# Block 0 of an interleaved attention and MLP kernel: a later load and later statistics for the third input tile, an undivided turn of the second, and one sum step moved behind a layer norm

## The chip, the cores and the metric

One Trainium2 chip (trn2), one of its cores. The metric is the device time of one launch in microseconds, as the median of several launches. Each launch also leaves a span, from the first to the last instruction of the program in the profile. The span is about 1.7 us shorter than the time in most launches, and it scatters less. All runs count as fast at a granted TensorE clock of 1.0, except one execution that is named where it occurs.

## The reference

Four layers on a [2048, 1024] bf16 residual: attention A, MLP B, attention A, MLP B, with the same weights both times.

```python
x = x + A(layernorm(x))     # qkv = x @ wqkv; 32 heads of 32; 8 keys at distance 0, 2, .. 14; softmax; @ wo
x = x + B(layernorm(x))     # (relu(x @ W_gate) * (x @ W_up)) @ W_down, hidden size 3584
x = x + A(layernorm(x))
x = x + B(layernorm(x))
```

## The kernel before

The 2048 rows are 16 tiles of 128, four to a block of 512. The program is a list of steps with a planned moment each. The list is sorted by that moment, and this gives every engine one order of instructions. The moment itself does nothing at run time. An engine runs its instructions in order, and so does SyncE, whose instructions are nearly all the loads and stores.

The opening, with block 0. V is computed first. Tile 0's products over the first half of the contraction start as soon as tile 0 is normalised and turned by PE transposes, then tile 1's, and so on.

```python
    def load_x(b, tiles=range(TPB)):
        for t in (b * TPB + i for i in tiles):
            if t == 0:
                sp_dma(x_tiles[t][:, 0:SLAB], ...)               # SyncE's queue
                nc.scalar.dma_start(x_tiles[t][:, SLAB:D], ...)  # ACT's queue
            elif t == 2:
                nc.scalar.dma_start(x_tiles[t][:], ...)
            else:
                sp_dma(x_tiles[t][:], ...)
    load_x(0, range(TPB - 1))
    ...
    load_slab(("v0", 0), qkv_half(2, 0))     # first V slab: two loads of 512 KB
    load_x(0, [TPB - 1])
    load_slab(("v0", 1), qkv_half(2, 1))
    ...
        scratch(13)                          # PE warm-up
        bn(0, 0); bn(0, 1); aggr(0)          # DVE statistics of tile 0, power on POOL
        act_square(2); act_mean(2)           # ACT statistics of tile 2
        bn(1, 0)
        apply(0, 0); apply(0, 1)             # DVE: tile 0 normalised
        turn(0)                              # PE: 8 transposes
        copy(0, "a", 0, 0, KC // 4)          # ACT: transposes to SBUF
        copy(0, "a", 0, KC // 4, KC // 2)
        bn(1, 1); aggr(1)
        copy(0, "v", 1)                      # DVE
        act_power(2)
        apply(1, 0); apply(1, 1)
        def second(h):
            turn(1, (h,))                    # 4 transposes
            if h == 0:
                copy(1, "v", 0)
                return
            copy(1, "v", 1)
            apply(2); act_square(3); act_mean(3); act_power(3); apply(3)
        ...
        def head():
            for kc in range(KC // 2):        # 4 times 8 products of tile 0
                if kc == KC // 2 - 1:
                    ln["second"](0)
                for c in range(KC):
                    prod(kc, c, 0, 1)
            ln["second"](1)                  # then tile 1's products
```

Around 180 us, the second layer norm (LN2) of block 0 and the logit sums of block 1 (steps of a product and an addition on DVE, `sums1`) share DVE. The sums are stored to DRAM and read back in another layout. The weight slabs of the MLP come in the same SyncE queue.

```python
    spread(sums1[6:10], t_fill + 1.4, 4.6)
    ...
            ev.append((at + 37.5, store_s(1, 1)))   # store of the scores' second half, waits for DVE
            ev.append((at + 40.5, load_s(1)))       # four loads of what it stored
    # slab_events: a weight slab is queued when a place in its ring of 5 should be free
            events.append((ends[i - RING] + 0.3 if i >= RING else 0.1 * i, ...))
```

Of the kernel before, what the change touches and what calls it, by code (L numbers as in the profile page):

```python
# [13 lines left out]
P = 128  # L14
# [6 lines left out]
KC = D // P  # L21
BLK = 512
TPB = BLK // P
# [13 lines left out]
def kernel(  # L37
# [11 lines left out]
    nc = tc.nc  # L49
# [13 lines left out]
    x_dram = A_x.flatten_outer_dims()  # L63
# [102 lines left out]
    x_tiles = []  # L166
# [4 lines left out]
    def load_x(b, tiles=range(TPB)):  # L171
        for t in (b * TPB + i for i in tiles):
            if t == 0:
                sp_dma(x_tiles[t][:, 0:SLAB], x_dram[t * P:(t + 1) * P, 0:SLAB])
                nc.scalar.dma_start(x_tiles[t][:, SLAB:D], x_dram[t * P:(t + 1) * P, SLAB:D])  # L175
            elif t == 2:
                nc.scalar.dma_start(x_tiles[t][:], x_dram[t * P:(t + 1) * P, :])
            else:
                sp_dma(x_tiles[t][:], x_dram[t * P:(t + 1) * P, :])

    load_x(0, range(TPB - 1))


    slab = {}
# [117 lines left out]
        return mv, rstd  # L302

    load_slab(("v0", 0), qkv_half(2, 0))
    load_x(0, [TPB - 1])
    load_slab(("v0", 1), qkv_half(2, 1))
    load_slab(("qk01", "q", 0), qkv_half(0, 0))

# [9 lines left out]
    def ln_first():  # L318
        hold = {"xnT": xnT_pool.tile([P, TPB, KC, P], BF16, tag="xnT", name="xnT_first")}
        xna = big_tile([P, TPB, D], "xn_first", True)  # L320
        last = {}

        def on(eng, f, *args, **kwargs):
            if eng == "v":
                dv(f, *args, **kwargs)
            elif eng in last:
                with tc.issue_after(last[eng]):
                    last[eng] = f(*args, **kwargs).ins  # L328
            else:
                last[eng] = f(*args, **kwargs).ins  # L330

        def small(name, bufs=4):
            return stat_pool.tile([P, 1], F32, tag="f" + name, name=name, bufs=bufs)

        mean, rstd, bst, sq = {}, {}, {}, {}

        def bn(t, half):
            if half == 0:
                bst[t] = stat_pool.tile([P, 2, 6], F32, tag="bst", name="bst")
            on("v", nc.vector.bn_stats, bst[t][:, half, :], x_tiles[t][:, half * SLAB:(half + 1) * SLAB])  # L340

        def aggr(t):
            mv = stat_pool.tile([P, 2], F32, tag="mv", name="mv", bufs=4)
            on("v", nc.vector.bn_aggr, mv[:], bst[t][:].rearrange("p a b -> p (a b)"))
            mean[t] = mv[:, 0:1]
            power(t, mv[:, 1:2], 1.0)

        def power(t, var, sign):
            rstd[t], vpe = small("rstd1"), small("vpe1")
            on("g", nc.gpsimd.tensor_scalar, vpe[:], var, sign, EPS, op0=ALU.mult, op1=ALU.add)  # L350
            on("g", nc.gpsimd.tensor_tensor, rstd[t][:], vpe[:], neg_half[:, 0:1], op=ALU.pow)

        def act_square(t):
            sq[t] = small("sq1")
            on("a", nc.scalar.activation, xna[:, t, :], x_tiles[t][:], ACT.Square, scale=float(D) ** -0.5,
               accum_out=sq[t][:])

        def act_mean(t):
            mn = small("mean1")
            on("a", nc.scalar.activation, xna[:, t, :], x_tiles[t][:], ACT.Identity, scale=1.0 / D, accum_out=mn[:])  # L360
            mean[t] = mn[:]

        def act_power(t):
            nvar = small("nvar1")
            on("v", nc.vector.scalar_tensor_tensor, nvar[:], mean[t], mean[t], sq[t][:], op0=ALU.mult, op1=ALU.subtract)
            power(t, nvar[:], -1.0)

        def apply(t, half=None):
            cols = slice(0, D) if half is None else slice(half * SLAB, (half + 1) * SLAB)
            on("v", nc.vector.tensor_scalar, xna[:, t, cols], x_tiles[t][:, cols], mean[t], rstd[t][:],  # L370
               op0=ALU.subtract, op1=ALU.mult)

        tps = {}

        def turn(t, halves=(0, 1)):
            if t in tps:
                pass
            elif t == 0:
                tps[t] = [psum.tile([P, KC // 2, P], BF16, tag="acc", name=f"tp{h}")[:] for h in range(2)]
            else:  # L380
                both = psum_l.tile([P, 2, KC, P], BF16, tag="L", name="tp_pair")
                tps[t] = [both[:, h, 0:KC // 2, :] for h in range(2)]
            for c in (h * (KC // 2) + i for h in halves for i in range(KC // 2)):
                with pe_group():
                    tail_pe[0] = nc.tensor.transpose(tps[t][c // (KC // 2)][:, c % (KC // 2), :],  # L385
                                                     xna[:, t, c * P:(c + 1) * P], ident[:]).ins

        def copy(t, eng, h, i0=0, i1=KC // 2):
            f = nc.vector.tensor_copy if eng == "v" else nc.scalar.copy
            on(eng, f, hold["xnT"][:, t, h * (KC // 2) + i0:h * (KC // 2) + i1, :], tps[t][h][:, i0:i1, :])  # L390

        warm = small("warm")
        on("a", nc.scalar.activation, warm[:], ones[:, 0:1], ACT.Identity)
        scratch(13)
        bn(0, 0)
        bn(0, 1)
        aggr(0)
        act_square(2)
        act_mean(2)
        bn(1, 0)  # L400
        apply(0, 0)
        apply(0, 1)
        turn(0)
        copy(0, "a", 0, 0, KC // 4)
        copy(0, "a", 0, KC // 4, KC // 2)
        bn(1, 1)
        aggr(1)
        copy(0, "v", 1)
        act_power(2)
        apply(1, 0)  # L410
        apply(1, 1)

        def second(h):
            turn(1, (h,))
            if h == 0:
                copy(1, "v", 0)
                return
            copy(1, "v", 1)
            apply(2)
            act_square(3)  # L420
            act_mean(3)
            act_power(3)
            apply(3)

        hold["second"], hold["last"] = second, last
        hold["later"] = {t: (lambda t=t: (turn(t), copy(t, "a", 0), copy(t, "v", 1))) for t in (2, 3)}
        return hold

# [22 lines left out]
    def v_first(ln):  # L451
        st = att[0]
        pairs, opened = {}, set()

        def prod(kc, c, t0, t1):
            part = t0 // 2
            if (part, c // 2) not in pairs:
                pairs[part, c // 2] = psum.tile([P, 2, BLK // 2], F32, tag="acc", name="acc_v")
            acc = pairs[part, c // 2][:, c % 2, (t0 % 2) * P:(t0 % 2 + t1 - t0) * P]
            with pe_group():  # L460
                mm(acc, lhsT=slab["v0", kc // (KC // 2)][:, kc % (KC // 2), c * P:(c + 1) * P],
                   rhs=ln["xnT"][:, t0:t1, kc, :], start=(part, c // 2) not in opened, stop=(kc == KC - 1),
                   skip_group_check=True)
            opened.add((part, c // 2))

        def head():
            st["vT"] = big_tile([P, KC, BLK], "vT_0", True)
            for kc in range(KC // 2):
                if kc == KC // 2 - 1:
                    ln["second"](0)  # L470
                for c in range(KC):
                    prod(kc, c, 0, 1)
            ln["second"](1)

        def first_half(t):
            def f():
                for c in range(KC):
                    if t == 2 and c == KC // 2:
                        ln["later"][3]()
                    for kc in range(KC // 2):  # L480
                        prod(kc, c, t, t + 1)
            return f

        def second_half(i, t0):
            def f():
                if (i, t0) == (2, 0):
                    ln["later"][2]()
                for c in (2 * i, 2 * i + 1):
                    for kc in range(KC // 2, KC):
                        prod(kc, c, t0, t0 + 2)  # L490
                tail_act[0] = nc.scalar.copy(st["vT"][:, 2 * i:2 * i + 2, t0 * P:(t0 + 2) * P],
                                             pairs.pop((t0 // 2, i))[:]).ins
            return f

        tail = [(GRP * (2 + 4 * part + 0.5 * i), second_half(i, 2 * part)) for part in range(2) for i in range(KC // 2)]
        return head, [(GRP, first_half(1)), (4 * GRP, first_half(2)), (5 * GRP, first_half(3))] + tail
# [471 lines left out]
    sums1 = prod_sum_steps(1)  # L968
    spread(sums1[:4], t_pv0 + 34.5, 4.5)
    spread(sums1[4:6], t_wo0 + 0.5, 2.5)  # L970
    spread(sums1[6:10], t_fill + 1.4, 4.6)
    spread(sums1[10:], t_gu0 + 2.6, 5.4)
    spread(load_v_steps(1), t_wo0 + 4.0, 7.0)
    ev.append((t_gu0 - 0.01, start_hidden))
# [107 lines left out]
```

## Time and profile before

| | us |
|---|---|
| time, median of 3 launches (lowest, highest) | 1617.87 (1617.67, 1618.37) |
| span of the profiled launch | 1616.4 |
| the same kernel in the later rounds beside the changed one, median of all 6 | 1618.20 (highest 1619.15) |

The page of the kernel before: span, busy time of the engines, and the chain of work that ended last.

```profile
span 1616.4 us, 18930 instructions
PE 1611.3 (100%) x7633; PEld 786.6 (49%) x7633; DVE 1137.1 (70%) x960; ACT 475.8 (29%) x968; POOL 180.4 (11%) x168
...
PE 99%; DMA 0%; ACT 0%; DVE 0%; issue 0%; ACTq 0%; DVEq 0%
```

PE is busy all the time and is the whole chain. The next view lists what PE waited for (total, times, longest, us).

```profile
PE scratch L132 <- DVE ones L310: 1.5, 1, 1.5
PE acc_v L132 <- ACT xnT_first L328: 0.4, 1, 0.4
```

The view lists no other wait of PE in 1616 us. PE's timeline of the opening (start us, length us, engine, line, operation, count, and in brackets idle time and its releaser):

```profile
6.97 0.72 PE L385 MATMUL tp<-ident,xn_first 128*128 128x128 bf16 x8
8.09 1.50 PE L132 MATMUL acc_v<-xnT_first,w_v 128*128 128x128 bf16 x24 [0.40 <-ACT xnT_first L328]
9.51 0.40 PE L385 MATMUL tp_pair<-ident,xn_first 128*128 128x128 bf16 x4
9.74 0.61 PE L132 MATMUL acc_v<-xnT_first,w_v 128*128 128x128 bf16 x8
10.64 3.59 PE L132 MATMUL acc_v<-xnT_first,w_v 128*128 128x128 bf16 x47
```

The 24, then 8 products of tile 0 have tile 1's first transposes between them, and tile 1's products begin at 10.64. ACT's timeline beside it shows why the first product came at 8.09. ACT ran tile 2's mean pass and turned to the copy only then:

```profile
6.63 1.06 ACT L328 ACTIVATE xn_first<-x 128x1024 bf16<-128x1024 bf16 x1
...
7.68 0.63 ACT L328 COPY xnT_first<-tp 128x256 bf16<-128x256 bf16 x2
```

DVE at LN2 of the last tile: the variance is ready at 181.0, but one product and one addition of the sums (`t` and `ac`, 2.29 us each) stand before the tile is normalised (`xn_b`).

```profile
180.85 0.15 DVE L106 TENSOR_SCALAR vpe<-mv 128x1 f32<-128x1 f32 x1
180.93 2.29 DVE L106 TENSOR_TENSOR t<-q,k 128x2048 f32<-128x2048 bf16 x1
183.14 2.29 DVE L106 TENSOR_TENSOR ac<-ac,t 128x2048 f32<-128x2048 f32 x1
185.35 0.54 DVE L106 TENSOR_SCALAR xn_b<-x,mv,rstd 128x1024 bf16<-128x1024 bf16 x1
```

### The profile page before, as it was taken

To read this page: it belongs to the slowest core of one execution; us is meant where nothing else is said; L and a number is where in the kernel's file an instruction comes from. 1 tells how busy PE (TensorE), PEld (TensorE's weight loads), DVE (VectorE), ACT (ScalarE), POOL (GpSimd) and SP (SyncE) were. 2 spreads that over 40 slices of the span, in tenths; PEclk is the share of its full clock that TensorE was granted. 3 is DMA by queue.
4 is the path that set the end of the run, shared out by engine and by line. 5 is a ranking of instruction groups with operands and counts; after the bars stand their busy time and mean duration, and the time that the engine had idled before them with its cause. 6 is when DMAs were issued, how large, how long until landed. Compare 5 with 4: busy or idle time off the path is not lost.

```text
span 1616.4 us, 18930 instructions
## 1 busy us (share of the span) xinstructions
PE 1611.3 (100%) x7633; PEld 786.6 (49%) x7633; DVE 1137.1 (70%) x960; ACT 475.8 (29%) x968; POOL 180.4 (11%) x168
## 2 busy tenths in 40 slices
PE   9999999999999999999999999999999999999999
PEld 6646544444444445444454444544445444444444
DVE  5999989996989698929489293893939939311211
ACT  5853312132116313603136031361313311131110
POOL 2400100010003002300053000530005100000000
PEclk9999999999999999999999999999999999999999
DMA  9868868697669766794847947479574794755452
GB/s 306 180 190 238 224 159 262 183 216 204 208 192 217 200 184 212 192 246 146 227 160 201 240 153 230 152 205 252 165 226 155 203 245 157 209 161 177 157 167 68
DMA packets 407448, 317.92 MB, mean 197 GB/s; under 512 B 166464, under 2 KB 387008, under 8 KB 406848
## 3 DMA queue, kind: packets, MB, share of 16 engines
q1 hardware_dynamic: 406784, 316.13, 69.9%
q8 instruction: 59, 0.97, 0.3%
q10 hardware_dynamic: 576, 0.59, 0.1%
q14 instruction: 29, 0.24, 0.0%
HBM read 266.29 MB, written 34.66 MB: 186 GB/s over the span
## 4 chain that ended last, share of the span: by engine, by line
PE 99%; DMA 0%; ACT 0%; DVE 0%; issue 0%; ACTq 0%; DVEq 0%
PE acc_u L132 24%; PE acc_g L132 24%; PE dacc L132 18%; PE acc_v L132 7%; PE acc_wo L132 7%; PE acc_k L132 7%; PE acc_q L132 7%; PE dacc_pair L132 6%; DMA x<-in_A_x_dram 0%; ACT xn_first L328 0%; PE tp_pair L385 0%; PE L L132 0%; DVE x L837 0%; DVE xnT_first L106 0%; ACTq L175 0%
## 5 line engine op out<-in xcount | busy, mean ns | idle before, releaser
L132 PE MATMUL acc_g<-xnT_b,w_g 128*128 128x512 bf16 x1792 | 423.3, 379 | 0.0
L132 PE MATMUL acc_u<-xnT_b,w_u 128*128 128x512 bf16 x1792 | 423.3, 379 | 0.0
L790 ACT ACTIVATE r<-acc_g 128x512 bf16<-128x512 f32 x224 | 133.5, 596 | 726.7 <-PE acc_g L132 701.6
L106 DVE TENSOR_TENSOR hT<-acc_u,r 128x512 bf16<-128x512 f32 x224 | 150.5, 685 | 240.7 <-PE acc_u L132 238.2
L132 PE MATMUL dacc<-w_d,hT 128*128 128x512 bf16 (+1 forms) x1400 | 301.9, 375 | 0.0
L132 PEld LDWEIGHTS <-hT 128*128 128x128 bf16 x1820 | 178.1, 98 | 208.9
L132 PEld LDWEIGHTS <-w_u 128*128 128x128 bf16 x1792 | 175.3, 98 | 211.5
L132 PEld LDWEIGHTS <-w_g 128*128 128x128 bf16 x1792 | 175.4, 98 | 211.4
L106 DVE TENSOR_TENSOR pv<-a,vhm 128x4096 bf16<-128x4096 bf16 x64 | 143.4, 2281 | 0.0
L837 DVE TENSOR_TENSOR x<-dacc,x 128x512 bf16<-128x512 f32 (+1 forms) x38 | 24.5, 672 | 154.2 <-PE dacc L132 154.2
L608 DVE TENSOR_TENSOR t<-q,k 128x2048 f32<-128x2048 bf16 x56 | 128.0, 2292 | 6.7 <-ACT k L543 4.6
L106 DVE TENSOR_TENSOR t<-q,k 128x2048 f32<-128x2048 bf16 x56 | 127.4, 2285 | 3.7 <-ACT k L543 2.6
L106 DVE TENSOR_TENSOR pv<-pv 128x1024 bf16<-128x1024 bf16 (+1 forms) x128 | 113.6, 947 | 0.0
L549 POOL COPY kh<-k 128x14 bf16<-128x14 bf16 x40 | 56.0, 1406 | 504.3 <-ACT k L543 504.3
L132 PE MATMUL acc_wo<-w_o,oT 128*128 128x512 bf16 x512 | 111.8, 379 | 0.0
L621 DVE TENSOR_TENSOR ac<-ac,t 128x2048 f32<-128x2048 f32 x48 | 109.6, 2284 | 0.3
L106 DVE TENSOR_TENSOR ac<-ac,t 128x2048 f32<-128x2048 f32 x48 | 109.5, 2282 | 0.0
L264 POOL TENSOR_TENSOR st_b<-st_b,neg_half 128x1 f32<-128x1 f32 x29 | 43.9, 1523 | 525.8 <-ACT st_b L263 525.7
L132 PE MATMUL dacc_pair<-w_d,hT 128*128 128x512 bf16 x420 | 95.9, 379 | 0.0
L132 PEld LDWEIGHTS <-oT 128*128 128x128 bf16 x512 | 50.0, 98 | 60.4
L259 ACT ACTIVATE xn_b<-x 128x1024 bf16<-128x1024 bf16 x29 | 30.3, 1045 | 129.1 <-DVE x L106 67.0
L446 ACT CAST vT<-acc_v 128x512 bf16<-128x512 f32 x56 | 32.8, 588 | 57.6 <-PE acc_v L132 56.6
(134 smaller groups left out, 1230.0 us busy)
## 6 DMA issues: line engine op xcount, KB each, us to landing
w_g<-in_B_W_gate_dram SPq DMA_DIRECT2D x56, 1024.0 KB, 7.4
w_u<-in_B_W_up_dram SPq DMA_DIRECT2D x56, 1024.0 KB, 5.5
w_d<-in_B_W_down_dram SPq DMA_DIRECT2D x48, 1024.0 KB, 5.7
w_o<-in_A_wo_dram SPq DMA_DIRECT2D x16, 1024.0 KB, 7.0
vhm<-v_d SPq DMA_DIRECT2D x32, 284.0 KB, 6.8
v_d<-vT SPq DMA_DIRECT2D x8, 1024.0 KB, 9.8
oT<-o_d SPq DMA_DIRECT2D x32, 256.0 KB, 4.5
w_d<-in_B_W_down_dram SPq DMA_DIRECT2D x16, 512.0 KB, 3.9
```

The source lines that it names most:

```text
L106: tail_dve[0] = f(*args, **kwargs).ins
L132: tail_pe[0] = nc.tensor.matmul(*args, **kwargs).ins
L259: nc.scalar.activation(xn, xt[:], ACT.Square, accum_out=sq)
L264: nc.gpsimd.tensor_tensor(rstd, vpe, neg_half[:, 0:1], op=ALU.pow)
L446: tail_act[0] = nc.scalar.copy(st["vT"][:, c, :], acc[:]).ins
L549: nc.gpsimd.tensor_copy(khalo[n][:, c, :], k[:, BLK:BLK + HALO])
L608: nc.vector.tensor_tensor(t[:], i0, i1, op=ALU.mult)
L621: nc.vector.tensor_tensor(o, ac[:], t[:], op=ALU.add)
L790: tail_act[0] = nc.scalar.activation(rs[j][:], acc[:], ACT.Relu).ins
L837: run = dv if n < NB - 2 else (lambda f, *args, **kwargs: f(*args, **kwargs))
```

## The change

Its intent is to let ACT's copy go at once (tile 2's statistics behind it, so its load may come later), to put the V weights ahead of tile 2 in the queue, to turn tile 1 in one piece, and to free LN2's last tile from a sum step. Tile 3's statistics move from ACT to DVE.

```diff
-            elif t == 2:
-                nc.scalar.dma_start(x_tiles[t][:], x_dram[t * P:(t + 1) * P, :])
...
-    load_x(0, range(TPB - 1))
+    load_x(0, [0, 1])
...
     load_slab(("v0", 0), qkv_half(2, 0))
-    load_x(0, [TPB - 1])
+    load_x(0, [2, 3])
...
         aggr(0)
-        act_square(2)
-        act_mean(2)
...
         copy(0, "a", 0, KC // 4, KC // 2)
+        act_square(2)
+        act_mean(2)
         bn(1, 1)
         aggr(1)
         copy(0, "v", 1)
-        act_power(2)
...
-        def second(h):
-            turn(1, (h,))
-            if h == 0:
-                copy(1, "v", 0)
-                return
+        def second():
+            turn(1)
+            copy(1, "v", 0)
             copy(1, "v", 1)
+            bn(3, 0)
+            act_power(2)
+            bn(3, 1)
+            aggr(3)
             apply(2)
-            act_square(3)
-            act_mean(3)
-            act_power(3)
             apply(3)
...
             for kc in range(KC // 2):
-                if kc == KC // 2 - 1:
-                    ln["second"](0)
                 for c in range(KC):
                     prod(kc, c, 0, 1)
-            ln["second"](1)
+            ln["second"]()
...
-    spread(sums1[6:10], t_fill + 1.4, 4.6)
+    spread(sums1[6:10], t_fill + 3.3, 4.0)
```

More of the change, by code (lines that the diff above doesn't have):

```diff
@@ L373, in ln_first, with turn @@
         tps = {}
-        def turn(t, halves=(0, 1)):
-            if t in tps:
-                pass
-            elif t == 0:
+        def turn(t):
+            if t == 0:
                 tps[t] = [psum.tile([P, KC // 2, P], BF16, tag="acc", name=f"tp{h}")[:] for h in range(2)]
@@ L382, in turn @@
                 tps[t] = [both[:, h, 0:KC // 2, :] for h in range(2)]
-            for c in (h * (KC // 2) + i for h in halves for i in range(KC // 2)):
+            for c in range(KC):
                 with pe_group():
```

## The prediction

> **What bounds the kernel.** TensorE. On the page PE is busy 1611.3 of 1616.4 us and the chain that ended last is 99% PE. PE waits twice: 1.5 us before its first warm-up matmul, 0.4 us before the first V product (on ACT's copy of tile 0's transposes). After 10.6 us the timeline has no PE gap. So only the first 10.7 us can pay, or a new stall can cost.
>
> **The opening now (timeline, us).** Tile 0's first four transposes end at 7.37, but ACT is in tile 2's mean pass (6.63 to 7.69), so its copy runs 7.68 to 8.04 and V starts at 8.09. A 128-column matmul takes 0.056. After 24 V products come tile 1's first four transposes (9.50), 8 products (to 10.19), a wait for DVE's copy (9.94 to 10.36), the other transposes (10.42), and tile 1's products at 10.64.
>
> **The change there.**
> - Tile 2's load goes behind the first V slab. Loads land at about 256 KB per 0.68 us (V halves 6.74 and 8.11, tile 3 8.79), so I expect tile 1 near 4.75, V halves 6.1 and 7.4, tile 2 8.1. None was PE's last wait.
> - Tile 2's two ACT passes follow the copies: the copy starts near 7.40, V near 7.81. Gain 0.28.
> - That gain is not kept. Tile 1's normalised halves still come at 9.41 and 9.78. The 32 products end at 9.59, eight transposes give results by 10.22, and only then DVE's copy (0.42) starts: the copies of the pair tile wait for all eight (tile 3: transposes end 17.87, copy 17.90). PE has nothing to do meanwhile; today eight V products cover it. Tile 1's products start near 10.73, against 10.64. Net cost 0.1.
> - Tile 3's statistics move to DVE (two passes of 0.65), tile 2's end later: applies end near 13.5 and 14.9, for turns at 14.2 and 17.3: no stall.
>
> **The sum step.** Now a product and an addition (2.29 each, from 180.93) stand before the fourth tile's apply (185.35); POOL's power beside them takes 2.55 against 0.55 for earlier tiles. Moved, the apply comes near 181.7 and its transposing load lands near 185.5, not 188.99. PE needs it at 190.29 and does not wait today: slack, no time. DVE loses about 0.7 idling for POOL, so the first gates come at 202.2, not 201.46; PE first needs that at 204.10. No PE effect.
>
> **Sum.** -0.28 (copy earlier) +0.38 (turn no longer covered) = +0.1 us, within scatter (1617.67 to 1618.37). The Trainium skill, "DMA: Bandwidth & Descriptors" (issuing engines are not separate DMA queues), says that DMAs of different engines run on the same 16 DMA engines and interleave; the landing rate here agrees, so moving the load reorders bytes and frees none.
>
> Predicted 1617.9 us, 8 in 10 between 1617.2 and 1618.5. Faster by over 2%: 0.005; within 2%: 0.99; slower: 0.005.
>
> **Signs that I am right:** ACT copy at 7.4, V at 7.8; a new PE wait of 0.5 to 0.7 us on DVE's copy of tile 1 between 10.0 and 10.75; first Q product within 0.2 of 23.88; first gate product within 0.2 of 190.29 without a wait; POOL's fourth power 0.55.
>
> **What would make it wrong:** copies not waiting for all eight transposes (then -0.15); tile 1 normalised earlier because its load is (up to -0.4); tile 2's late statistics holding its turn at 14.2 (up to +0.7); DVE's delay reaching PE's accumulators near 204 (+0.5).

## More of the kernel before

Last, DMA traffic between 3.5 and 6.0 us, by queue (packets, MB, share of 16 engines). q1 is SyncE's queue and q10 is ACT's.

```profile
DMA packets 539, 0.98 MB, mean 393 GB/s; under 512 B 51, under 2 KB 67, under 8 KB 539
...
q1 hardware_dynamic: 384, 0.72, 78.3%
q10 hardware_dynamic: 155, 0.26, 27.4%
```

SyncE's queue at 230 us: the store of the scores (`s_d`), the four loads of what it stored, a load of Q, and then the up-weight slab that PE needs next.

```profile
230.70 0.34 SPq L121 DMA_DIRECT2D s_d<-s  x1
...
233.90 4.38 SPq L121 DMA_DIRECT2D s<-s_d  x4
...
239.88 0.39 SPq L121 DMA_DIRECT2D w_u<-in_B_W_up_dram  x1
```

## The result

| | before | after |
|---|---|---|
| time, median of 6 (lowest, highest), us | 1618.20 (1617.67, 1619.15) | 1619.26 (1618.48, 1619.68) |
| ratio after to before, 95% interval | | 1.0005 (0.9992 to 1.0018): same |

A ratio is the mean time of one kernel's fast runs over that of the other's of the same rounds, so it is not quite the ratio of the medians. The class "within 2%" was right, but 1619.26 lies 0.76 us above the stated range. The interval of the timed rounds does not establish a loss. All executions taken together point to one: the mean span is 1617.47 in 16 executions of the kernel after (these six, e3 and e15) and 1616.48 in 55 of the kernel before. The profiles show where it arises, because a place where PE stands still is seen in them directly.

The page after:

```profile
span 1617.9 us, 18928 instructions
PE 1610.5 (100%) x7633; PEld 786.0 (49%) x7633; DVE 1138.6 (70%) x962; ACT 473.4 (29%) x964; POOL 178.7 (11%) x168
...
PE 96%; DVE 2%; DMA 2%; SPq 0%; issue 0%; DVEq 0%
```

The chain now has 2% DVE and 2% DMA, which it did not have before. PE's waits after:

```profile
PE scratch L132 <- DVE ones L308: 1.5, 1, 1.5
PE acc_u L132 <- DMA w_u<-in_B_W_up_dram: 0.9, 1, 0.9
PE acc_v L132 <- DMA w_v<-in_A_wqkv_dram: 0.7, 2, 0.4
PE tp L381 <- DVE xn_first L106: 0.7, 1, 0.7
PE acc_v L132 <- DVE xnT_first L106: 0.5, 1, 0.5
```

The wait for `tp` costs nothing in itself. The warm-up matmuls ended earlier in this launch, and PE then waited for tile 0 to be normalised. Three others are new: the V slab (twice), DVE's copy of tile 1, and an up-weight slab. The opening in PE's timeline after:

```profile
6.53 0.72 PE L381 MATMUL tp<-ident,xn_first 128*128 128x128 bf16 x8 [0.68 <-DVE xn_first L106]
7.66 1.07 PE L132 MATMUL acc_v<-xnT_first,w_v 128*128 128x128 bf16 x16 [0.42 <-DMA w_v<-in_A_wqkv_dram]
9.02 1.07 PE L132 MATMUL acc_v<-xnT_first,w_v 128*128 128x128 bf16 x16 [0.29 <-DMA w_v<-in_A_wqkv_dram]
9.92 0.61 PE L381 MATMUL tp_pair<-ident,xn_first 128*128 128x128 bf16 x8
11.05 3.19 PE L132 MATMUL acc_v<-xnT_first,w_v 128*128 128x128 bf16 x43 [0.52 <-DVE xnT_first L106]
```

Tile 1's products begin at 11.05, not 10.64, although tile 0's input landed 0.5 us earlier in this launch (3.7 against 4.2 us). ACT's copy no longer waits for anything of tile 2. It starts at 6.96, 0.43 after the first transpose, where before it was 0.71 after it:

```profile
6.96 0.65 ACT L326 COPY xnT_first<-tp 128x256 bf16<-128x256 bf16 x2 [4.22 <-PE tp L381]
```

DVE at LN2's last tile:

```profile
181.29 0.15 DVE L106 TENSOR_SCALAR vpe<-mv 128x1 f32<-128x1 f32 x1
182.11 0.55 DVE L106 TENSOR_SCALAR xn_b<-x,mv,rstd 128x1024 bf16<-128x1024 bf16 x1 [0.66 <-POOL rstd L299]
182.57 2.28 DVE L106 TENSOR_TENSOR t<-q,k 128x2048 f32<-128x2048 bf16 x1
```

The tile is normalised 0.82 us after the variance's instruction starts, as predicted, but DVE idles 0.66 us for POOL first, and the sums come after that. SyncE's queue after:

```profile
232.00 0.34 SPq L121 DMA_DIRECT2D s_d<-s  x1
...
235.19 4.94 SPq L121 DMA_DIRECT2D s<-s_d  x4
...
241.76 0.39 SPq L121 DMA_DIRECT2D w_u<-in_B_W_up_dram  x1
```

Everything in it is later, the up slab by 1.88 us. Of this, 0.45 us is the later opening (first Q product at 24.33 instead of 23.88). PE needs that slab next, and stands still:

```profile
248.83 1.90 PE L132 MATMUL acc_u<-xnT_b,w_u 128*128 128x512 bf16 x8 [0.95 <-DMA w_u<-in_B_W_up_dram]
```

The chain of waits says the same from the other side. These are its pieces in order (start, length, what):

```profile
229.68 2.30 DVE s L106
...
232.00 3.17 DMA s_d<-s
...
241.76 7.02 DMA w_u<-in_B_W_up_dram
```

It runs from DVE's last sum through its store, SyncE's queue and the slab's load (landing at 248.78) into the matmuls at 248.83 shown above. Last, the DMA traffic between 3.5 and 6.0 us after:

```profile
DMA packets 219, 0.41 MB, mean 162 GB/s; under 512 B 21, under 2 KB 21, under 8 KB 219
...
q1 hardware_dynamic: 219, 0.41, 79.7%
```

Less than half of what was moved before, and SyncE's queue alone has work.

### The profile page after: what moved, and what is told of

Same layout as the page of the kernel before. It is cut to its first block, busy times and chain, and to the rows that moved or that the text cites. A ratio compares the mean times of both kernels' runs of the same rounds, so it can differ in the third digit from the quotient of the medians.

```text
span 1617.9 us, 18928 instructions
## 1 busy us (share of the span) xinstructions
PE 1610.5 (100%) x7633; PEld 786.0 (49%) x7633; DVE 1138.6 (70%) x962; ACT 473.4 (29%) x964; POOL 178.7 (11%) x168
## 4 chain that ended last, share of the span: by engine, by line
PE 96%; DVE 2%; DMA 2%; SPq 0%; issue 0%; DVEq 0%
PE acc_u L132 22%; PE acc_g L132 22%; PE dacc L132 18%; PE acc_k L132 7%; PE acc_q L132 7%; PE acc_wo L132 7%; PE acc_v L132 7%; PE dacc_pair L132 6%; DVE ac L106 1%; DVE t L106 1%; DMA w_g<-in_B_W_gate_dram 0%; SPq L121 0%; DMA w_u<-in_B_W_up_dram 0%; DMA w_v<-in_A_wqkv_dram 0%; DMA s_d<-s 0%
```

## The experiments

Two theories from the first comparison. Theory Q: the sum step makes DVE late, the scores' store late, and through SyncE's order the up slab late. Theory V, later R: the opening is set by the V slab, and its landing suffers when tile 2's load leaves ACT's queue. The rivals are that the front alone is the loss, that the loss is scatter of launches, and that bytes land at one fixed rate in the order of issue (the prediction).

To compare profiles of different launches, three numbers are read from each trace: the first Q product counted from the last landing of tile 0 ("Q"), the scores' store counted from the first Q product, and the last matmul counted from the first Q product. The last is 1589.41 where PE has no gap after the opening. What it has over that is the stall at the up slab. A landing is the last semaphore update of a load in the trace.

| kernel (profile of) | tile 2's load | turn of tile 1 | second V half, after tile 0 | KB in 3.5 to 6.0 us | Q | store after Q | stall at 248 |
|---|---|---|---|---|---|---|---|
| before | ACT | split | 3.91 | 983 | 19.68 | 206.82 | 0 |
| e5, before again | ACT | split | 4.78 | 926 | 19.71 | 206.83 | 0.15 |
| e16, before again | ACT | split | 5.01 | 802 | 19.87 | 206.82 | 0.39 |
| e6, sum step alone | ACT | split | 4.23 | 942 | 19.73 | 207.68 | 0.55 |
| after | behind V | whole | 5.26 | 406 | 20.61 | 207.67 | 1.13 |
| e3, after again | behind V | whole | 5.64 | 469 | 21.00 | 207.68 | 0.82 |
| e15, after again | behind V | whole | 4.41 | 799 | 19.81 | 207.68 | 0.54 |
| e2, front alone | behind V | whole | 5.33 | 442 | 20.70 | 206.82 | 0 |
| e4, after, up slab first | behind V | whole | 5.41 | 379 | 20.76 | 207.68 | 0 |
| e7, after, load on ACT | ACT | whole | 4.70 | 863 | 20.01 | 207.67 | 1.09 |
| e8, after, split turn | behind V | split | 4.87 | 537 | 20.22 | 207.69 | 0.85 |
| e9, after, V half on ACT | behind V | whole | 3.56 | 948 | 19.89 | 207.69 | 0.95 |
| e10, three edits | ACT | split | 4.83 | 936 | 19.72 | 206.83 | 0 |
| e13, the same again | ACT | split | 4.79 | 953 | 19.71 | 206.82 | 0 |
| e11, e10 with load moved | behind V | split | 4.31 | 619 | 19.90 | 206.84 | 0 |
| e12, the same again | behind V | split | 4.36 | 705 | 19.76 | 206.83 | 0 |
| e14, the same again | behind V | split | 4.94 | 429 | 20.30 | 206.82 | 0 |

Every run below gave the reference's result, was timed in 5 rounds, and is classed "same" against before (the intervals are about 0.13% to either side, 2 us).

### The two halves of the change, and the change again (e1, e2, e3, e6, e15)

e1 and e6 are the kernel before with one line of the change. e2 is the kernel after without it.

```diff
-    spread(sums1[6:10], t_fill + 1.4, 4.6)
+    spread(sums1[6:10], t_fill + 3.3, 4.0)
```

> The kernel before with only the sum step moved behind LN2. Theory Q (the SyncE queue carries DVE's lateness to PE): DVE runs about 0.85 us later against PE from LN2 to the second half's store of the scores, so that store, the four loads behind it and then the up-weight slab in the same queue are issued over 1 us later; PE stalls 0.6 to 1.1 us at the up product near 248.4 us, the first up product of the fifth slab, and the time is +0.6 to +1.1 us. Rival F (the front alone is the loss): no PE gap near 248 us, time within 0.2 us of before. Rival N (scatter of launches): the gap comes and goes between runs of any kernel.

e1's profile fell into an execution of 4806 us, in which PE worked at about a quarter of its pace. The run lists a clock of 1.0, but its trace holds no clock record at all (nor does that of e15, which was fast). It tells nothing of the stall. Its loads of the first 6 us, with tile 2's on ACT's queue, moved 848 KB between 3.5 and 6.0 us, which agrees with the other kernels of that load order in the table. Its four other executions had a mean span of 1617.12 us, against 1616.64 of before in the same rounds.

> The sum-step-alone kernel once more, because its profile fell into an execution at a third of the speed. Theory Q: PE gap of 0.5 to 0.9 us at the up product near 247.5 to 248.5 us, while the first Q product stands as in the kernel before of the same launch kind. If the gap is absent, the sum step alone isn't enough.

e6: the store comes 0.86 us later after the first Q product, and PE's only new wait that counts is one of 0.4 us for the up-weight slab. Counted by the last matmul, the stall is 0.55 us. The mean span was 1616.72 against 1616.46.

> The kernel after with the sum step where it was. Theory Q: DVE and PE shift alike, no PE gap near 248 us, time 0 to +0.5 us by the front alone (0.1 if the loads land as in the trace of before, 0.45 if they come in the slow way of the trace of after). Rival F: the whole loss of about 0.9 us. The opening's DMA: if the slow landing of the V slabs (7.6 and 9.0 instead of 6.7 and 8.1 us) belongs to the new load order it is seen here again; if it is scatter it is not.

e2: no gap at 248 us, V halves at 7.52 and 8.84, the first Q 20.70 after tile 0's landing. The mean span was 1617.08 against 1616.64. So the front alone costs too, and not through the fifth up slab. PE waited 0.8 us in all for the two V halves.

> The kernel after, unchanged, for more rounds and a second profile. Theory Q: a PE gap of about 1.1 us at the up product near 248.8 us again, time +0.7 to +1.5 us. Rival N: the gap or the slow landing of the first V slabs is gone in this profile.

> The kernel after, third time. Scores' store 207.7 us after the first Q, PE gap of 0.5 to 1.1 us near 248 us; first product of tile 1 at least 2.9 us after the first V product; few bytes (380 to 710 KB) between 3.5 and 6.0 us by theory R; mean span 0.8 to 1.3 us over before.

e3: the gap again (0.82), V halves at 8.05 and 9.39, mean span 1617.84 against 1616.64. e15: the gap again (0.54), but V landed in time (6.65 and 8.16) and 799 KB flowed, against what theory R expected. This launch shows what the front does when the V slab is there. PE's timeline of it:

```profile
7.41 1.95 PE L132 MATMUL acc_v<-xnT_first,w_v 128*128 128x128 bf16 x32
9.19 0.61 PE L381 MATMUL tp_pair<-ident,xn_first 128*128 128x128 bf16 x8
10.32 3.69 PE L132 MATMUL acc_v<-xnT_first,w_v 128*128 128x128 bf16 x48 [0.51 <-DVE xnT_first L106]
```

V starts 3.66 us after tile 0's landing, where it took 3.89 to 4.03 in the four profiles with the front of before. From there to tile 1's products it is 2.91 us, with 0.51 of idle time before them. The first Q is at 19.81, against a mean of 19.75: the predicted +0.1. The mean span of e15 was 1617.24 against 1616.36.

### The up slab ahead of the scores' store (e4)

```diff
-            events.append((ends[i - RING] + 0.3 if i >= RING else 0.1 * i, ...))
+            early = 3.6 if key == ("u", 0, 4) else 0.0
+            events.append((ends[i - RING] + 0.3 - early if i >= RING else 0.1 * i, ...))
-            ev.append((at + 37.5, store_s(1, 1)))
+            ev.append((at + 38.4, store_s(1, 1)))
```

> The kernel after, but the fifth up-weight slab is put in the SyncE queue ahead of the store of the scores' second half, so it no longer waits behind that store and the four loads. Theory Q: it is issued near 230.5 us instead of 241.8 and lands before 240, PE has no gap near 248 us, and what is left is the front's cost, 0 to +0.5 us against before. Rival F: time as the kernel after. Rival B (bandwidth, not queue order): the slab lands early but the score loads land later, DVE's softmax waits and PE stalls elsewhere, time not better than after.

SyncE's queue in e4: the up slab goes first, at a moment in which SyncE only waited for DVE before.

```profile
230.56 0.37 SPq L121 DMA_DIRECT2D w_u<-in_B_W_up_dram  x1
231.92 0.34 SPq L121 DMA_DIRECT2D s_d<-s  x1
...
237.68 3.37 SPq L121 DMA_DIRECT2D s<-s_d  x4
```

The store is as late as in the kernel after (207.68 after the first Q), the four score loads come 2.5 us later than there, and PE has no gap: 1589.41. So the stall was the order of one queue and not DVE's lateness by itself, nor bandwidth (rival B). The mean span was still 1617.40 against 1616.64, which is more than the 0 to 0.5 us expected: it holds the front, and an end of the span 0.5 us longer, of which more below.

### Tile 2's load back on ACT's queue, and the turn split again (e7, e8)

```diff
 e7: the kernel after
+            elif t == 2:
+                nc.scalar.dma_start(x_tiles[t][:], x_dram[t * P:(t + 1) * P, :])
-    load_x(0, [0, 1])
+    load_x(0, [0, 1, 2])
-    load_x(0, [2, 3])
+    load_x(0, [3])
 e8: the kernel after
+        def second(h):
+            turn(1, (h,))
+            if h == 0:
+                copy(1, "v", 0)
+                return
             copy(1, "v", 1)
...
+                if kc == KC // 2 - 1:
+                    ln["second"](0)
```

> The kernel after with tile 2's load alone put back on the ACT queue at the front; its statistics stay behind the copies and the turn stays merged. Theory V: the V halves land no later than in the kernel after (7.5 to 8.0 and 8.8 to 9.4 us) although 256 KB more stand before them, because two queues move more during the slow stretch between 3.7 and 6 us than SyncE's queue alone; first Q within 0.2 us of after's 24.2 to 24.75. Rival (bytes in order: what stands before the V slab delays it at full rate): V halves 0.65 us later than in the kernel after, first Q near 24.9 to 25.4. The gap near 248 us stays (0.6 to 1.1).

> The kernel after with tile 1's turn split in two again around the last eight products of tile 0, as before. If the merged turn's uncovered copy costs what the profile shows (PE idle 0.52 us plus its own length against 0.07 before), tile 1's products start 0.3 to 0.45 us earlier than in the kernel after at the same V landing (after: 2.08 us from the landing of the second V half to the first product of tile 1; here near 1.7), and the first Q 0.3 to 0.45 us earlier. Rival (the V landing hides it): no change. The gap near 248 us stays (0.6 to 1.1).

e7: the V halves land at 7.56 and 8.89, no later than in the kernel after, as theory V expected and against the rival. 863 KB flow in the stretch instead of 379 to 469 in the four slow profiles with that turn, and PE does not wait for V at all. What is left is the whole turn: 2.97 us from the first V product to tile 1's (7.99 to 10.96), as in e15 (2.91) and e9 (2.91). e8: with the split turn it is 2.46 us (7.89 to 10.35), as in e6. In the three profiles of before it is 2.54 to 2.74. The cleanest measure is from the landing of the second V half, in profiles where PE waited for it: 2.07 to 2.08 us to tile 1's products with the whole turn (after, e2, e3), 1.62 to 1.67 with the split one (e16, e10, e13, e14). So the whole turn costs about 0.45 us there. Where the first V product comes early, the split turn saves less: e10, e13 and e11 take 2.80 to 2.81 us from it, because PE then waits 0.12 to 0.18 us for the second V half or for tile 1 to be normalised. The mean spans were 1617.22 (e7) and 1617.34 (e8) against 1616.46. e8's first Q is still late (20.22), because the second V slab also landed late (12.64) and PE waited 0.17 us for it.

### A kernel measured against itself (e5, e16)

> The kernel before, unchanged, run as a candidate: a second profile of it and the scatter of times of one and the same kernel (ratio 1.000). Theory V (the V slab, not the load order of tile 2, sets the opening): in a launch where tile 0's input lands near 3.5 us, the V halves land near 7.45 and 8.8 us here too, as in the slow-clock profile of the sum-step-alone kernel, and tile 1's products start near 10.2 to 10.6 us. Rival (the slow V landing belongs to the new load order): V halves at 6.7 and 8.1 us, or earlier. No PE gap near 248 us, the fifth up slab landing 0 to 0.5 us ahead of its need.

> The kernel before, third profile. Scores' store 206.8 us after the first Q, PE gap near 247 us 0 to 0.2; 850 to 990 KB between 3.5 and 6.0 us by theory R; first product of tile 1 2.5 us after the first V product; ratio 1.000.

Mean spans 1616.42 against 1616.46 and 1616.34 against 1616.36. The opening of one and the same kernel scatters: tile 0 lands at 3.7 to 4.2 us and the second V half at 8.1 to 9.1. The up slab has no reserve here either: e5 and e16 already stall by 0.15 and 0.39 us, where no gap and at most 0.2 were expected. e16's 802 KB also lie under the 850 to 990 that theory R expected.

### Half of the V slab on ACT's queue (e9)

```diff
         if key[0] == "v0":
             for i in range(2):
                 rows = slice(i * (KC // 4), (i + 1) * (KC // 4))
+                if key == ("v0", 0) and i == 0:
+                    nc.scalar.dma_start(tv[:, rows, :], src[:, rows, :])
+                    continue
                 sp_dma(tv[:, rows, :], src[:, rows, :])
```

> The kernel after, but the first 512 KB of the V slab come from the ACT queue, behind tile 0's half; the second 512 KB stay in SyncE's. Theory R (between 3.5 and 6 us one queue alone moves little, two move more): the 16 engines move over 700 KB between 3.5 and 6.0 us (after: 406, before: 983) and the second V half lands near 8.0 us or earlier instead of 8.8 to 9.4. Rival T (the V slab's own rows are slow to read until about 6 us whichever queue asks): under 550 KB in that stretch, V halves as in the kernel after. The merged turn and the gap near 248 us stay.

Traffic of e9 between 3.5 and 6.0 us, the same load order otherwise as in the kernel after:

```profile
DMA packets 495, 0.95 MB, mean 379 GB/s; under 512 B 32, under 2 KB 32, under 8 KB 495
...
q10 hardware_dynamic: 257, 0.49, 53.1%
q1 hardware_dynamic: 238, 0.45, 47.7%
```

Each queue moves as much as SyncE's did alone in the kernel after (0.41 MB), so together it is 0.95 MB. The V halves land at 5.62 and 7.14. The V slab's own data are therefore not slow to read (rival T falls), and a second queue with work is enough. This is one profile. The mean span, 1617.12 against 1616.41, keeps the whole turn and the stall at 248 (0.95).

### Three edits, and the load move by itself (e10, e13, e11, e12, e14)

e10 is the kernel before with e4's edit and with tile 2's passes behind the copies. Load, split turn and sum step stay as before.

```diff
-        act_square(2)
-        act_mean(2)
         bn(1, 0)
...
         copy(0, "a", 0, KC // 4, KC // 2)
+        act_square(2)
+        act_mean(2)
...
-        act_power(2)
         apply(1, 0)
...
             copy(1, "v", 1)
+            act_power(2)
             apply(2)
```

> The kernel before with three edits only: tile 2's two ACT passes stand behind tile 0's copies (load still on the ACT queue, turn still split), its power behind tile 1's copies, and the fifth up slab is queued ahead of the scores' store; the sum step stays where it was. Expected: ACT's copy starts when tile 0's transposes end, V starts about 0.3 us earlier against tile 0's landing than before (4.1 us after it), tile 1's products and the first Q 0.2 to 0.4 us earlier (Q 19.65 after tile 0's landing instead of 19.9), no PE gap near 248 us (last matmul 1589.41 after the first Q). In all -0.2 to -0.5 us against before, which the timed rounds can hardly show.

> The three-edit kernel again (load on the ACT queue). Theory R: 850 to 990 KB between 3.5 and 6.0 us, second V half at most 4.9 us after tile 0's last landing; first Q near 19.7 to 19.9 us after tile 0's last landing; no gap near 248; last matmul to end of span 3.08 us; mean span 0.2 to 0.5 us under before.

The gap at 248 us is gone in both, but the front gains nothing: the first Q is at 19.72 and 19.71. V starts earlier and then waits for the second V half (0.15 us in e10, which landed 4.83 after tile 0). The expected 0.2 to 0.4 us was wrong. Mean spans were 1616.04 against 1616.41, and 1616.26 against 1616.36. That is at best 0.1 to 0.4 us (0.2 to 0.5 was expected) and not established by the rounds. It is no version that beats the kernel before for certain.

e11, e12 and e14 are e10 with tile 2's load moved as in the change:

```diff
-            elif t == 2:
-                nc.scalar.dma_start(x_tiles[t][:], x_dram[t * P:(t + 1) * P, :])
-    load_x(0, range(TPB - 1))
+    load_x(0, [0, 1])
-    load_x(0, [TPB - 1])
+    load_x(0, [2, 3])
```

> The same as the run before it with the load of tile 2 alone moved behind the V slab, as in the change: the load move by itself. Theory R: fewer than 600 KB land between 3.5 and 6.0 us against 850 to 980, the V halves land 0.4 to 1.0 us later after tile 0's landing although 256 KB less stand before them, PE waits for the V slab, first Q 0.3 to 0.8 us later than in that run. Rival (as predicted blind): V halves 0.65 us earlier, first Q unchanged.

> The load move by itself once more, because the one profile of it caught the shortest of its five executions (span 1616.6, the others 1617.1 to 1617.5; the kernel it differs from by that load alone had 1615.8 to 1616.3). Theory R: in a typical execution fewer than 550 KB land between 3.5 and 6.0 us, the V halves land near 7.5 and 8.9 us or later, PE waits for them, and the first Q comes 0.5 to 1.2 us after the 23.5 us seen in both; mean span again 0.6 us or more over before. If the profile shows V in time, Q near 23.5 and a span over 1617, the loss is not in the opening and the load move's cost stays unexplained.

> The same with tile 2's load behind V. Theory R: 380 to 710 KB between 3.5 and 6.0 us. Scatter theory: no lower than in the run before it. The end of the span again 3.6 us after the last matmul if that belongs to the kernel, 3.08 if to the launch. Mean span 0.5 to 1.2 us over the run before it.

619, 705 and 429 KB flow in the stretch, against 936 and 953 without the move. The first Q is at 19.90, 19.76 and 20.30 instead of 19.71. So the move costs 0.05 to 0.6 us here, by the launch. Counted from the start of the span the difference is smaller: the first Q is at 23.55, 23.72 and 24.37, against 23.52 and 23.96 without the move, because tile 0 landed a little earlier with it. In e14 PE lost most of it not to the first V slab (a wait of 0.13 us) but to the second (0.32), whose halves landed at 11.71 and 13.08. The numbers that e11 and e12 had to show for the V halves (0.4 to 1.0 us later, PE waiting) did not come: they landed at 6.51 and 7.96, and at 7.02 and 8.32. The mean spans (1617.22, 1616.74, 1617.16) are not a clean measure, because the profiles of these three and of e4 end 3.6 to 3.8 us after the last matmul instead of 3.1. The very last store lands 2.0 to 2.1 us after its issue where it takes 1.57 in the others. Only kernels with both the moved load and the reordered up slab have it. Why is open.

## Why the prediction was wrong

**Right.** PE bounds the kernel, only its first 10.7 us or a new stall can matter, and the class is "within 2%". ACT's copy gains about 0.3 us when V is there (e15: V 3.66 after tile 0's landing, 3.89 to 4.03 before; predicted 0.28). The whole turn leaves PE without work while DVE copies: 2.91 us from the first V product to tile 1's, predicted 10.73 - 7.81 = 2.92. Where V landed in time (e15) the sum of the two was +0.06 us on the first Q product, predicted +0.1. The tile's apply at LN2 followed its variance by 0.82 us, and POOL's power took 0.55 instead of 2.55. The next step, the tile's transposing load, did not come as predicted: SyncE was still issuing other transfers and issued it only at 185.06, 2.4 us after the apply, so it landed at 189.00 and not near 185.5. That cost nothing, because PE had no wait there.

**Wrong, first term: "tile 1 near 4.75, V halves 6.1 and 7.4, tile 2 8.1. None was PE's last wait."** The prediction took the landing rate seen in the kernel before, 256 KB per 0.68 us, for a property of the 16 engines, and let 256 KB less stand before V. Nine profiles have the load behind V and all of V on SyncE's queue (e9 is left out, with half of V on the other queue). In them the second V half never came before 7.96, and in five of the nine not before 8.84. In the stretch from 3.5 to 6.0 us those nine moved 379 to 799 KB (four of them under 450). The seven with the load on ACT's queue moved 802 to 983, and their second V half came at 7.92 to 9.07, mean 8.59. With the load behind V it is 7.96 to 9.39, mean 8.68. So the V slab came no earlier, where the prediction had it 0.7 us earlier. What did come earlier was tile 1 (4.05 to 4.62 instead of 4.70 to 5.23) and perhaps tile 0 (mean 3.73 instead of 3.98, with ranges that overlap); neither helped where V was the last input that PE needed. In the five profiles with the whole front of the change the first Q product comes at 20.58 on average after tile 0, against 19.75 in the four with the front of before. Instead of +0.1 this is +0.8, with a spread of 1.2 between launches. PE's waits for V are seen in three of the five (after, e2, e3). In e15 V was in time, and in e4 the warm-up held tile 0's transposes back until 7.05, so the first V product came late without a wait for V.

No run contradicts the sentence of the Trainium skill, "DMA: Bandwidth & Descriptors" (Issuing engines are not separate DMA queues), that DMAs of different engines run on the same 16 DMA engines and interleave: in the kernel before, 0.72 MB of SyncE's queue and 0.26 MB of ACT's moved in the same stretch. But the conclusion drawn from it, that moving a load "frees none" and costs none, did not follow. The same page (Queues, rings and completion order) says that each DMA engine takes turns between the queues that it has work for. That would let a second queue fill the pauses of the first. e9 fits this and shows that a second queue suffices. It is not the whole story, though: with tile 2 on ACT's queue, SyncE's own queue moved more (565 to 722 KB, mean 681) than it did alone (mean 531), and its longest packets took 0.3 to 0.8 us instead of 0.8 to 1.6. Why one queue is slow just there was not tested.

**Wrong, second term: "DVE loses about 0.7 ... PE first needs that at 204.10. No PE effect."** DVE's loss was 0.86 (206.82 to 207.68, the same in all profiles), of which 0.66 is the wait for POOL. The size was nearly right, and PE's accumulators indeed never waited. The step that failed is "no PE effect": it looked for DVE's lateness only where PE reads from DVE. The path went over SyncE: DVE's last sum at 230, its store, four loads that wait for the store to land, and the up slab behind them, which in the kernel before lands at 223.01 to 223.71 after the first Q where it is needed at about 223.4. There was no slack. The stall was 0.54 to 1.13 us in the seven profiles with the moved sum step and the old queue order, 0 to 0.39 in the four without it, and 0 in all six with the slab queued first.

**The sum.** Predicted -0.28 + 0.38 = +0.1. Measured in the last matmul of the three profiles each: 1614.44 after (mean of 1614.86, 1614.97, 1613.50) against 1613.33 (1613.29, 1612.96, 1613.73), which is +1.1. Of this +0.65 is the stall at the up slab (means 0.83 and 0.18). The rest, +0.47, is the opening: +0.72 counted from tile 0's landing, less 0.25 because tile 0 landed earlier in the launches of after. Whether that was chance or came of the moved load was not tested; if it came of the load, the opening's cost by the clock is the 0.47.

**A range that was too narrow.** 1617.2 to 1618.5 was drawn around three launches that agreed within 0.7 us. Launches of the kernel before alone later went from 1617.63 to 1619.91. One source is PE's warm-up. The 13 matmuls took 5.50 us in the profile of before and 4.33 in that of after. The Trainium skill, "TensorE: Matmul & The Clock Gate" (What's actually happening), says that the gate's activity window is free-running, so the moment of warming differs between runs of one kernel. The traces agree: in seven of the profiles tile 0's transposes start at 6.97 to 7.05, with no idle time behind the warm-up matmuls, and in the others at 6.3 to 6.9 (in e13 at 7.06, after a wait for DVE).

## What to carry to other kernels

Follow a delay not only to the engine that bounds the kernel, but through every queue that runs in order: a store that waits for a late engine holds back all loads behind it, and the slack that counts is that of the next load. A load that waits for nothing should stand ahead of a store that waits. In the first 6 us of these launches, a landing rate read while two queues had work was no rate for one queue, so treat the move of an early load between queues as a change of bandwidth until a trace says otherwise.

## What the Trainium skill lacked or had wrong

- "DMA: Bandwidth & Descriptors" (Rules for kernel authors) says that spreading DMAs over issuing engines for bandwidth doesn't help. Here it did in the first 6 us of a launch: 379 to 799 KB between 3.5 and 6.0 us in nine profiles with SyncE's queue nearly alone, 802 to 983 KB in seven with tile 2's load on ACT's queue, 948 KB in one with half of the V slab there. It was not issue time that was saved: in the kernel after, SyncE had issued both V loads by 2.7 us, and they landed at 7.62 and 8.97. Later one queue was enough: the same nine moved 352 to 410 KB in the one us from 7 to 8.
- The same page gives the order within a queue, but it does not warn that a DMA waiting on the issuing engine delays the unrelated ones behind it. Here 0.86 us of DVE raised PE's stall from 0 to 0.39 us to 0.54 to 1.13 us, and queueing one slab ahead of the store took it to 0.
- "TensorE: Matmul & The Clock Gate" (Seeing it yourself) tells of clock-gate records that can't be trusted and of a gate stuck at a quarter for over 50 us. It does not cover a whole launch like that: one of e1's five took 4806 us instead of 1618, with PE at a quarter of its pace, and its trace holds no clock record.
